# Moving the row-sum products of the norm behind the output products of their slot

## The chip, the cores and the metric

One Trainium2 chip, one core. The metric is the device time of one execution in microseconds (us). Timed runs of the kernel before gave a median of 982.25 us (979.91 to 983.06, 3 runs).

Names of engines in the lines of the profile: PE is TensorE's products, PEld its weight loads, DVE is VectorE, ACT is ScalarE, POOL is GpSimd.

## The reference

A Fourier filter along the sequence, then a gated feed-forward network with an RMS norm in front:

```
X = rfft(x, axis=1)                      # x: 8 x 3008 x 256
y = irfft(X * (filt_r + i filt_i))       # per batch
rms = sqrt(mean(y*y, axis=-1) + 1e-6)
xn  = y / rms * rms_g
out = (silu(xn @ w_gate) * (xn @ w_val)) @ w_out     # 256 -> 1536 -> 256
```

The norm needs, for each of the 3008 positions of each of the 8 batches, the sum of 256 squares. The kernel takes these sums on TensorE, as products of the squares with a column of ones. They are the row-sum products of the title.

## The kernel before

After a start-up, the kernel runs 576 slots: 8 batches, 6 tiles (m) of up to 512 positions, and 12 column blocks (jt) of the hidden layer. A slot is `gv` (gate and value products, into pg and pv) for the slot itself and `down` (output products, into po) for the slot two before it. Between them stand the units of the Fourier filter of later batches, which are laid into the slots by a plan. One of these units is `q_unit`, the row sums:

```python
psM = ctx.enter_context(tc.tile_pool(name="psM", bufs=1, space=bass.MemoryType.PSUM))
psB = ctx.enter_context(tc.tile_pool(name="psB", bufs=1, space=bass.MemoryType.PSUM))
...
def b_unit(b, i):                        # filter products, into psb: the one buffer of psB
    ps = bank(3 if b else (0, 1, 3)[i % 3], "psb").rearrange("p (a d) -> p a d", a=2)
    ...
        if b > 1:
            nc.vector.tensor_tensor(out=s1, in0=ps, in1=f1, op=ALU.mult)      # L223
            st[b]["s"][i] = (s1, s2, ps, f2)
            return
    ...
def swap_unit(b, i, h):                  # reads psb one (h = 0) and two (h = 1) slots later
    ...
    nc.vector.tensor_tensor(out=s2[a], in0=ps[e], in1=f2[e], op=ALU.mult)     # L243
    if h:
        ...
        nc.gpsimd.tensor_tensor(out=s, in0=s1, in1=s2, op=ALU.add)            # L246
...
def q_unit(b, m):
    sq = st[b]["sq"].pop(m)
    ps = psB.tile([P, 4], FP32, tag="mb", name="psq")     # the same buffer as psb
    for q in range(4):
        for dh in range(2):
            nc.tensor.matmul(ps[:, q:q + 1], sq[:, dh, ts(q, P)], ones,       # L304
                             start=(dh == 0), stop=(dh == 1))
    ...
    nc.vector.tensor_scalar(out=u, in0=ps, ...)                               # L308
    nc.gpsimd.tensor_tensor(out=rho, in0=u, in1=mhalf, op=ALU.pow)            # L310
...
for i in range(len(items) + 4):          # the slots
    if i < len(items):
        gv(*items[i])
    for fn, a in plan.get(i, ()):        # units: psa, psq, psi, psb, psn ...
        fn(*a)
    if 2 <= i < len(items) + 2:
        down(*items[i - 2])              # po; at jt == 11 also the copies of po to o
```

For batches from 2 on, psb is written every fourth slot. It has three readers on DVE, in that slot and the next two: a product with f1, and two "swap" products, each of one half of psb with f2 (h = 0, then h = 1, the second swap). psq comes in the slot after. psq of batches 1 to 6 therefore meets psb of the batch after, 36 times. Other units: psa (first stage of the transform, of two batches later), psi (inverse filter products), psn (last stage of the inverse).

## Time and profile before

| | before |
|---|---|
| time, median | 982.25 us |
| busy: PE, DVE, ACT, POOL | 91%, 68%, 64%, 38% of the span |
| weight loads of psq that waited for DVE's second swap | 36 times, 32.0 us |
| last pv to psq, start to start, waited / not waited | 0.78 / 0.216 us |

The head of the page of before, with the busy time, share of the span and number of instructions of each engine:

```profile
span 986.1 us, 17361 instructions
## 1 busy us (share of the span) xinstructions
PE 896.9 (91%) x6095; PEld 555.3 (56%) x6095; DVE 669.7 (68%) x1047; ACT 632.9 (64%) x1066; POOL 377.2 (38%) x325
```

TensorE is the limit, so what counts is where it stands still. The lists of waits of before, of the products and of the weight loads, tell who waited for whom: total us, times, longest.

```profile
engine line waited for: us in total, times, longest us
PE psq L304 <- DVE s L243: 14.7, 36, 0.5
...
PE psi L255 <- POOL s L246: 2.5, 7, 0.5
...
PE psb L215 <- DVE u L308: 0.4, 1, 0.4
```

```profile
engine line waited for: us in total, times, longest us
PEld L304 <- DVE s L243: 32.0, 36, 0.9
```

The timeline of before shows one of the 36 (start, duration, engine, line, operation; in brackets the idle time before it and what ended it):

```profile
319.04 0.59 PE L382 MATMUL pv<-xn,wv 128*128 128x512 f16 x2
...
319.30 0.68 DVE L243 TENSOR_TENSOR s<-psb,fi 64x512 f16<-64x512 f32 x1
320.01 0.69 DVE L387 TENSOR_TENSOR hh<-pv,sg 128x512 f16<-128x512 f32 x1
320.03 0.27 PEld L304 LDWEIGHTS <-sq 128*128 128x128 f16 x8 [0.89 <-DVE s L243]
320.04 0.35 PE L304 MATMUL psq<-ones,sq 128*128 128x1 f16 x8 [0.40 <-DVE s L243]
...
320.25 0.38 PE L194 MATMUL psa<-xc,wa 128*128 128x512 f16 x1
320.25 0.53 PEld L398 LDWEIGHTS <-hh 128*128 128x128 f16 x4
320.47 0.60 PE L398 MATMUL po<-wo,hh 128*128 128x256 f16 x4
```

The swap ends at 319.98 and psq starts at 320.04. The two pv products start 0.22 us apart, so the next product could have started at about 319.48. The wait costs 0.56 us, more than the 0.40 us that the list books, because the list counts from the end of a product and a pipelined successor starts before that end. Meanwhile the psa and po products, which need nothing from the swap, stand in line behind psq. The chain of waits of before says the same: it leaves TensorE here and runs over ACT and DVE.

```profile
317.94 0.61 ACT sg L386
318.55 0.02 issue
318.57 0.69 DVE hh L387
319.26 0.03 issue
319.30 0.69 DVE s L243
319.99 0.05 issue
320.04 0.35 PE psq L304 x8
320.39 0.24 PE psa L194
320.63 0.44 PE po L398 x4
```

### The profile page before, as it was taken

To read this page: it belongs to the slowest core of one execution; us is meant where nothing else is said; L and a number is where in the kernel's file an instruction comes from. 1 tells how busy PE (TensorE), PEld (TensorE's weight loads), DVE (VectorE), ACT (ScalarE), POOL (GpSimd) and SP (SyncE) were. 2 spreads that over 40 slices of the span, in tenths; PEclk is the share of its full clock that TensorE was granted. 3 is DMA by queue.
4 is the path that set the end of the run, shared out by engine and by line. 5 is a ranking of instruction groups with operands and counts; after the bars stand their busy time and mean duration, and the time that the engine had idled before them with its cause. 6 is when DMAs were issued, how large, how long until landed. Compare 5 with 4: busy or idle time off the path is not lost.

```text
span 986.1 us, 17361 instructions
## 1 busy us (share of the span) xinstructions
PE 896.9 (91%) x6095; PEld 555.3 (56%) x6095; DVE 669.7 (68%) x1047; ACT 632.9 (64%) x1066; POOL 377.2 (38%) x325
## 2 busy tenths in 40 slices
PE   3446978899999999999999999999999999999997
PEld 1223545565555656666666656666666666666654
DVE  6623444577777777777777878777777878555554
ACT  7333666677756776677766776577756765566543
POOL 3564334435441445325552445234431444033200
PEclk8556999999999999999999999999999999999999
DMA  8869574663457444764456434732345323422211
GB/s 194 150 124 175 130 167 99 149 173 86 92 111 164 85 101 92 162 129 90 91 117 158 108 78 92 173 101 73 76 106 130 87 60 68 116 44 62 44 44 41
DMA packets 94839, 106.99 MB, mean 108 GB/s; under 512 B 17112, under 2 KB 69464, under 8 KB 94560
## 3 DMA queue, kind: packets, MB, share of 16 engines
q1 hardware_dynamic: 85104, 87.92, 37.5%
q0 software_dynamic: 9552, 17.77, 11.8%
q8 instruction: 48, 0.79, 0.4%
q14 instruction: 39, 0.32, 0.1%
q10 hardware_dynamic: 96, 0.20, 0.1%
HBM read 70.62 MB, written 49.90 MB: 122 GB/s over the span
## 4 chain that ended last, share of the span: by engine, by line
PE 72%; DVE 8%; DMA 7%; issue 4%; ACT 4%; POOL 3%; SPq 0%; DVEq 0%; POOLq 0%; ACTq 0%
PE po L398 22%; PE pg L382 21%; PE pv L382 19%; DVE hh L387 4%; DVE s L243 3%; PE psi L255 3%; ACT sg L386 3%; PE psb L215 2%; DMA fi<-in_filt_i_dram 2%; PE psn L286 2%; PE psa L194 2%; PE psq L304 1%; DMA z_tmp<-t 1%; DVE o L404 1%; DMA wv<-in_moe_w_val_dram 1%
## 5 line engine op out<-in xcount | busy, mean ns | idle before, releaser
L387 DVE TENSOR_TENSOR hh<-pv,sg 128x512 f16<-128x512 f32 (+1 forms) x576 | 391.7, 680 | 253.8 <-ACT sg L386 106.5
L386 ACT ACTIVATE sg<-pg 128x512 f16<-128x512 f32 (+1 forms) x576 | 338.7, 588 | 237.2 <-PE pg L382 221.0
L398 PE MATMUL po<-wo,hh 128*128 128x256 f16 x2304 | 350.3, 273 | 1.7
L382 PE MATMUL pg<-xn,wg 128*128 128x512 f16 (+1 forms) x1152 | 341.2, 378 | 0.0
L382 PE MATMUL pv<-xn,wv 128*128 128x512 f16 (+1 forms) x1152 | 340.7, 378 | 0.0
L398 PEld LDWEIGHTS <-hh 128*128 128x128 f16 x2304 | 219.6, 98 | 107.1 <-issue 14.5
L246 POOL TENSOR_TENSOR s<-s,s 128x512 f16<-128x512 f16 x96 | 110.6, 1152 | 377.4 <-DVE s L243 340.5
L382 PEld LDWEIGHTS <-wv 128*128 128x128 f16 x1152 | 113.5, 99 | 133.3 <-issue 4.4
L367 POOL TENSOR_TENSOR xn<-y,rb 128x1024 f16<-128x1024 f32 x46 | 132.1, 2871 | 53.6 <-DMA rb<-r_tmp 53.6
L243 DVE TENSOR_TENSOR s<-psb,fi 64x512 f16<-64x512 f32 x192 | 132.1, 688 | 6.0
L382 PEld LDWEIGHTS <-wg 128*128 128x128 f16 x1152 | 113.0, 98 | 14.2 <-issue 0.6
L260 ACT ACTIVATE t<-psi 96x512 f16<-96x512 f32 x128 | 75.6, 592 | 24.7 <-PE psi L255 13.3
L196 ACT ACTIVATE t<-psa 128x512 f16<-128x512 f32 x96 | 56.4, 602 | 29.7 <-PE psa L194 24.3
L291 ACT ACTIVATE y<-psn,gsb 128x512 f32<-128x512 f32 x94 | 64.6, 687 | 13.7 <-PE psn L286 5.8
L310 POOL TENSOR_TENSOR rho<-u,mhalf 128x4 f32<-128x4 f32 x48 | 49.0, 1022 | 56.0 <-DVE u L308 55.9
L255 PEld LDWEIGHTS <-wi 128*128 128x128 f16 x320 | 33.5, 106 | 58.7 <-issue 22.4
L223 DVE TENSOR_TENSOR s<-psb,fr 128x512 f16<-128x512 f32 x96 | 65.4, 682 | 0.7 <-PE psb L215 0.2
L215 PE MATMUL psb<-t,wb 96*128 96x256 f16 x256 | 52.6, 290 | 7.6 <-DMA t<-z_tmp 6.1
L296 ACT ACTIVATE sq<-psn 128x512 f16<-128x512 f32 x94 | 55.6, 592 | 0.0
L255 PE MATMUL psi<-s,wi 128*128 128x256 f16 x256 | 46.6, 274 | 6.9 <-ACT sq L296 3.9
L194 PE MATMUL psa<-xc,wa 128*128 128x512 f16 x96 | 37.5, 405 | 16.7 <-DMA xc<-in_x_dram 8.8
L286 PEld LDWEIGHTS <-t 128*128 128x128 f16 x376 | 29.3, 99 | 22.5 <-issue 1.9
(60 smaller groups left out, 387.9 us busy)
## 6 DMA issues: line engine op xcount, KB each, us to landing
out_dram<-o SPq DMA_DIRECT2D x88, 256.0 KB, 3.3
z_tmp<-t SPq DMA_DIRECT2D x128, 96.0 KB, 2.3
t<-z_tmp SPq DMA_DIRECT2D x32, 384.0 KB, 5.0
g_tmp<-t SPq DMA_DIRECT2D x64, 192.0 KB, 3.2
t<-g_tmp SPq DMA_DIRECT2D x126, 96.0 KB, 2.7
rb<-r_tmp SPq DMA_DIRECT2D x46, 256.0 KB, 4.2
xc<-in_x_dram POOLq DMA_DIRECT2D x56, 192.0 KB, 5.9
out_dram<-o SPq DMA_DIRECT2D x8, 192.0 KB, 3.0
```

The costliest lines, as they stand in the source:

```text
L215: nc.tensor.matmul(ps[:, u, :], wb[:, k, :], st[b]["t2"][k // KC][:, k % KC, :], start=True, stop=True)
L223: nc.vector.tensor_tensor(out=s1, in0=ps, in1=f1, op=ALU.mult)
L243: nc.vector.tensor_tensor(out=s2[a], in0=ps[e], in1=f2[e], op=ALU.mult)
L246: nc.gpsimd.tensor_tensor(out=s, in0=s1, in1=s2, op=ALU.add)
L255: nc.tensor.matmul(ps[:, u, :], wi[:, 2 * i + u, q, :], ss[q][:, u, :], start=(q == 0), stop=(q == n - 1))
L260: nc.scalar.activation(out=st[b]["t3"][c][:, 2 * r:2 * r + 2, :], in_=ps[0:KR], func=AXT.Copy)
L291: nc.scalar.activation(out=y[:, dh, :], in_=ps, func=AXT.Identity, scale=gsb[:, dh:dh + 1])
L367: nc.gpsimd.tensor_tensor(out=xv, in0=yv, in1=rv.unsqueeze(1).to_broadcast([P, 2, 4, P]), op=ALU.mult)
L382: nc.tensor.matmul(ps[:, 0:w], wt[:, dt_, ts(jt, P)], xn[:, dt_, 0:w], start=(dt_ == 0), stop=(dt_ == 1))
L386: nc.scalar.activation(out=sg[:, 0:w], in_=pg[:, 0:w], func=AXT.Silu)
L387: nc.vector.tensor_tensor(out=hh[:, 0:w], in0=pv[:, 0:w], in1=sg[:, 0:w], op=ALU.mult)
L398: nc.tensor.matmul(po[s4 // 2][:, s4 % 2, :], hh[:, ts(s4, P)], wo[:, jt, :], start=(jt == 0 and s4 % 2 == 0), stop=(jt == JT - 1 and s4 % ...
```

## The change

The intent is to let ready work pass the row sums: psq and its DVE reader u are emitted at the end of the slot, behind the other units and behind po.

```diff
-        plan = {}
+        plan, late = {}, {}
 
         def at(slot, fn, *a):
-            todo = plan.setdefault(slot, [])
+            todo = (late if fn == q_unit else plan).setdefault(slot, [])
...
                 down(*items[i - 2])
                 if items[i - 2][2] == JT - 1:
                     stores[i + 1] = items[i - 2][:2]
+            for fn, a in late.get(i, ()):
+                fn(*a)
             if i in stores:
                 o_store(*stores[i])
```

No instruction is added or removed.

## The prediction

> **What bounds it now.** TensorE: the page has PE busy 91% of the span, DVE 68%, ACT 64%; the chain of waits is 72% PE. From 300 us on the timeline shows it streaming almost without a gap: a slot is two pg and two pv products (0.22 us from start to start), extra units, then four po products (0.44 us together). The largest wait of this steady part is the one that the change touches: in the list of waits, weight loads of the row-sum products (psq) waited 32.0 us for DVE s (the second swap product), 36 times; PE is booked idle 14.7 us there. "PSUM — Partial Sum Buffer" of the Trainium skill, section Terms, says that a bank is 2 KiB per partition; psq and the filter product psb share the one such buffer of their pool, so psq may not write before the swap has read psb. The trace agrees: the swap ends at 319.98, psq starts at 320.04.
>
> **What the wait costs.** From the start of the last pv to the start of psq it takes 0.78 us where psq waits and 0.216 us where it doesn't. So each of the 36 waits costs 0.56 us: 20 us, 2.1% of the run.
>
> **What the change does.** No instruction is added or removed. psq and its DVE consumer u go behind the slot's other units and po. Work of 0.44 us (po), or 0.66 us where the slot also holds a psa, fills the wait.
> - 20 of the 36 slots (batches 1 to 5) hold a psa: 0.56 us each, 11.2 us.
> - Batch 6 has none: four slots keep 0.13 us, gain 0.43 each, 1.7 us.
> - In 12 slots po also ends a tile. There u now stands behind the DVE copy of o (0.68 us, or 0.42 + 0.41), and the next slot's psb needs the buffer that u reads. hh (0.69), copy and u (0.15) end 1.5 to 1.7 us after the swap, so psb starts almost when it did: gain 0.05 to 0.2 each, 1.4 us, and a new wait "psb for DVE u", 0.2 to 0.4 us each.
> - Batch 1: psi waits for the POOL addition (1.15 us), partly behind xn (2.87 us), whose start hangs on the DMA of rho. PE coming earlier waits there: minus 1.5 us.
> - Batch 0: two slots (near 131 and 178 us) hold a psb of batch 1, now in front of psq, which then waits for two DVE products of 0.68 us: minus 1.0 and 0.8 us; another slot wins 0.2.
>
> Later rho costs little elsewhere: xn is needed several slots later, and the first use of rho (95 us) waits for POOL, held by weight DMAs.
>
> **Sum.** 11.2 + 1.7 + 1.4 - 1.5 - 1.6 = about 11 us of the 20. Predicted 971 us, range 965 to 976. Faster by over 2% (below about 963) 0.07, within 2% 0.92, slower 0.01.
>
> **What would show it.** In the list of waits "psq for DVE s" falls from 14.7 us to below 3 (weight loads: from 32 to below 10); "psb for DVE u" rises from 0.4 to 3 to 5 us. Busy times and counts stay. In a slot with psa the next pg starts 0.56 us sooner after the last pv. The gain is even over batches 2 to 6, small in batch 1, zero in batch 7, negative in batch 0.
>
> **What would make it wrong.** If ACT or DVE, which caught up during these waits, become the next limit, the gain is smaller. If u behind the copy delays psb less than worked out, it goes towards 15 to 18 us. If psq between po and the next pg exposes weight loads that were hidden, some 0.1 us for each of 48 units is lost.

## The result, and the profile after

The kernel after took 969.0 us (967.03 to 969.92, 4 runs) beside 982.55 us for the kernel before (979.91 to 983.06, 4 runs). The ratio is 0.9865, with a 95% interval of 0.984 to 0.9889: 1.35% less time, clear of noise but within 2%. Ratios here are the mean time of one kernel's fast runs over that of the other's of the same rounds, so not quite the ratio of the quoted medians. Run again later, the kernel after took 967.41 us (5 runs), a ratio of 0.9852 (0.9826 to 0.9878).

The head of the page of after:

```profile
span 966.1 us, 17361 instructions
## 1 busy us (share of the span) xinstructions
PE 884.5 (92%) x6095; PEld 553.0 (57%) x6095; DVE 668.8 (69%) x1047; ACT 632.9 (66%) x1066; POOL 376.8 (39%) x325
```

In the list of the products' waits of after, psq no longer waits for L243 at all. Two short waits for L237, in batch 0, are new. The list of the weight loads keeps a remainder:

```profile
engine line waited for: us in total, times, longest us
...
PE psi L255 <- POOL s L246: 3.4, 9, 0.6
...
PE psq L304 <- DVE s L237: 1.0, 2, 0.7
```

```profile
PEld L304 <- DVE s L243: 3.9, 16, 0.3
```

The same slot in the timeline of after:

```profile
313.51 0.59 PE L382 MATMUL pv<-xn,wv 128*128 128x512 f16 x2
...
313.77 0.68 DVE L243 TENSOR_TENSOR s<-psb,fi 64x512 f16<-64x512 f32 x1
313.95 0.38 PE L194 MATMUL psa<-xc,wa 128*128 128x512 f16 x1
...
314.16 0.60 PE L398 MATMUL po<-wo,hh 128*128 128x256 f16 x4
...
314.60 0.34 PE L304 MATMUL psq<-ones,sq 128*128 128x1 f16 x8
...
314.80 0.59 PE L382 MATMUL pg<-xn,wg 128*128 128x512 f16 x2
```

The swap still ends about 0.94 us after the first pv starts, as before (319.98 - 319.04 and 314.45 - 313.51). But psa and po now run in that time, and psq finds its buffer free. From the first pv of this slot to the first pg of the next it takes 1.29 us here; before it took 1.86 us (the next pg of before starts at 320.90). The chain of waits of after stays on TensorE:

```profile
313.68 0.43 PE pv L382 x2
314.11 0.22 PE psa L194
314.33 0.44 PE po L398 x4
314.76 0.18 PE psq L304 x8
314.94 0.45 PE pg L382 x2
```

To place the gain, I took from each trace the start of the gate activation (sg) of every slot and subtracted. A second trace of each kernel shows how far such a stage repeats:

| stage (slots) | before | before, again | after | after, again |
|---|---|---|---|---|
| 0 to 40 | 88.3 | 84.1 | 82.0 | 80.2 |
| 40 to 54 | 27.59 | 27.60 | 28.38 | 28.54 |
| 54 to 72 | 28.94 | 28.93 | 28.63 | 28.45 |
| 72 to 144 | 113.52 | 113.50 | 111.47 | 111.35 |
| 144 to 216 | 109.91 | 109.90 | 106.93 | 106.92 |
| 216 to 288 | 109.90 | 109.91 | 106.93 | 106.92 |
| 288 to 360 | 109.91 | 109.89 | 106.93 | 106.93 |
| 360 to 432 | 108.61 | 108.61 | 105.95 | 105.94 |
| 432 to 504 | 103.68 | 103.67 | 102.15 | 102.13 |
| 504 to 575 | 94.38 | 94.38 | 94.24 | 94.24 |

From slot 72 on, stages repeat within 0.15 us, and from slot 144 within 0.02 us. The gains there add up to 15.3 us (2.05 + 2.98 + 2.97 + 2.98 + 2.66 + 1.53 + 0.14). The first 40 slots wait for loads from memory and scatter by several us between executions of one kernel; the trace of before with its span of 986.1 us had an unluckily long start. Part of it is TensorE's granted clock: in the trace of before it is 0.63 of full speed from 142 to 145 us and 0.66 from 151 to 154 us, and products start up to 0.43 us apart there instead of 0.22. The second trace of before has one such stretch there, those of after have none; whether the change has to do with that is not shown. So the 20 us between the two spans is not the gain. The timed 13 to 15 us is, and what the first 72 slots contribute to it can't be told to better than some 2 us.

### The profile page after: what moved, and what is told of

Read it like the earlier page. It is cut to its first block, busy times and chain, and to the rows that moved or that the text cites. A ratio compares the mean times of both kernels' runs of the same rounds, so it can differ in the third digit from the quotient of the medians.

```text
span 966.1 us, 17361 instructions
## 1 busy us (share of the span) xinstructions
PE 884.5 (92%) x6095; PEld 553.0 (57%) x6095; DVE 668.8 (69%) x1047; ACT 632.9 (66%) x1066; POOL 376.8 (39%) x325
## 4 chain that ended last, share of the span: by engine, by line
PE 77%; DMA 8%; issue 5%; POOL 4%; DVE 4%; ACT 2%; SPq 0%; POOLq 0%; DVEq 0%; ACTq 0%
PE po L398 23%; PE pg L382 22%; PE pv L382 21%; PE psi L255 3%; PE psb L215 2%; DMA fi<-in_filt_i_dram 2%; PE psn L286 2%; PE psa L194 2%; DMA rb<-r_tmp 2%; DVE hh L387 1%; POOL s L246 1%; DVE o L404 1%; PE psq L304 1%; DMA wv<-in_moe_w_val_dram 1%; DMA xc<-in_x_dram 1%
## 5 line engine op out<-in xcount | busy, mean ns | idle before, releaser
L246 POOL TENSOR_TENSOR s<-s,s 128x512 f16<-128x512 f16 x96 | 110.7, 1153 | 358.7 <-DVE s L243 296.8
L243 DVE TENSOR_TENSOR s<-psb,fi 64x512 f16<-64x512 f32 x192 | 132.1, 688 | 6.0
L382 PEld LDWEIGHTS <-wg 128*128 128x128 f16 x1152 | 109.2, 98 | 12.6 <-issue 0.6
```

The source lines that it names most:

```text
L382: nc.tensor.matmul(ps[:, 0:w], wt[:, dt_, ts(jt, P)], xn[:, dt_, 0:w], start=(dt_ == 0), stop=(dt_ == 1))
```

## The experiments

The expectations below speak of "batches 2 to 5" and 106.1, 106.9 or 106.3 us each. That holds for the slots of batches 2 to 4; the slots of batch 5 (360 to 432) take about 1 us less in every kernel, which I had overlooked, so I compare batches 2 to 4.

My theory: the gain is the wait for psb's buffer, filled by the products that were moved in front of psq, and nothing else. Two rivals: the new place of psq or po in the stream of TensorE is worth something of its own (weight loads hidden or bared, buffers released sooner); or the gain comes from other engines' work starting earlier.

The traces of before and after speak against the second rival. Taken slot by slot, from the first pg to the first pg of the next slot, in batches 2 to 4 (slots 144 to 360) only the six slots of each batch with a psq are shorter: by 0.57 us with a psa (0.61 in the tile of 448 columns), by 0.43 without. The slots right behind the two in which po ends a tile are 0.14 and 0.08 us longer. No other slot differs by more than 0.01 us, and the second traces give the same.

### Take away the wait, keep the order

```diff
-                todo.insert(0, (fn, a))
+                todo.insert(len([f for f, _ in todo if f == swap_unit]), (fn, a))
...
-                    at(s0 + 2, swap_unit, b, i, 1)
+                    at(s0 + 1, swap_unit, b, i, 1)
```

This is the kernel before with the second swap one slot earlier, right behind the first (the changed insert keeps the two in order). psq stays in front of po.

> The order of before, psq in front of po, but the second swap product moved one slot earlier, behind the first, so that the bank is free long before psq. If the wait for the bank is the whole cost: psq waits for DVE s fall from 36 to none, all 20 us of the waits are won (more than the change's 13), and psi of batch 2 waits less for the POOL addition too: about 960 us. If instead the gain of the change came from where po or psq stand in the TensorE stream (weight loads, an earlier release of buffers), nothing is won: 980 us or more. If DVE with three products in one slot becomes the limit: above 985 us.

Measured: 956.14 us (4 runs), ratio 0.9723 (0.9685 to 0.9761). A second set gave 956.19 us (5 runs), ratio 0.9734 (0.9703 to 0.9765):

> The order of before with the early second swap once more, the fastest version so far, beside the other on one chip: 955 to 958 us, batches 2 to 5 at 106.1 us each, the stage of slots 40 to 54 at 27.6 us as in before (psq of batch 0 in front).

The list of the products' waits holds no line of psq for L243 and none of psi for the POOL addition (L246); the weight loads of psq keep 1.2 us for L243, 7 times. (The second trace has one wait for the addition, 0.8 us, before slot 72.) The stage of slots 72 to 144 takes 106.42 us and each of the next three 106.1 us, 0.8 us less than after. The second trace repeats this to 0.02 us. Its stage of slots 40 to 54 took 28.68 us instead of the expected 27.6, with the order of before: that stage too can differ by a us by chance.

The cause is shown: with the order of before untouched, freeing the buffer earlier wins all that the change won and more. This run also starts the addition on POOL earlier, so the slots have to be told apart. From slot 72 on it wins 24.7 us: 19.7 us in the 34 slots with a psq, 0.57 us in each (0.61 with 448 columns); 3.6 us in other slots of batch 1, where psi no longer waits for POOL; 1.4 us in others, which I did not follow up. DVE with three products in one slot was no limit.

### Half of the move

```diff
+            for fn, a in late.get(i, ()):
+                fn(*a)
             if 2 <= i < len(items) + 2:
                 down(*items[i - 2])
...
-            for fn, a in late.get(i, ()):
-                fn(*a)
```

> psq behind the slot's other units but still in front of po: half of the change. If the gain is just the work that stands between and fills the wait: 20 slots with a psa gain 0.22 us each, 4.4 us, and batch 0 loses about 1.6 as in the change: about 979 to 980 us, and in the trace psq still waits 0.56 us in slots without psa and 0.34 us with. If only the place behind po matters: 982 to 984 us. If any move backwards is enough: 969 us.

Measured: 980.94 us (4 runs), ratio 0.9978 (0.9936 to 1.0021), a little above the 979 to 980 expected and not to be told from before by its time. The trace tells it: the list of waits has all 36 again, shorter in total than the 14.7 us of before.

```profile
PE psq L304 <- DVE s L243: 10.3, 36, 0.5
```

In slots with a psa, psa to psq takes 0.56 us from start to start, where the psa stream itself takes 0.22: a wait of 0.34 us, as expected. Without psa, pv to psq takes 0.78 us as before. Batches 2 to 4 take 108.98 us each, 0.92 us less than before; four times 0.22 is 0.88. So the gain is the amount of work placed in front of psq, up to the length of the wait.

### Both together: the place of psq when there is nothing to fill

This is the change with the earlier second swap, both diffs from above.

> The change and the earlier second swap together. Theory: the move behind po is worth only the wait that it fills; with the bank free early there is none to fill, so the place of psq is worth nothing: the run's time within 2 us of the run with the early swap alone (956 us), batches 2 to 5 within 0.2 us of its 106.1 us each. Rival: standing between po and pg has a gain (or a cost) of its own, such as weight loads hidden or bared: batches differ by 0.6 us (0.1 us in each of six slots) or more, in either direction.

Measured: 958.46 us (5 runs), ratio 0.9758 (0.9733 to 0.9783). Batches 2 to 4 take 106.34 us each against 106.13 with the early swap alone. The move on top of the early swap wins nothing; it costs about 0.2 us per batch. The bounds that I had set (0.2 us per batch, 2 us in all) were both just missed, so I looked for those 0.2 us. In the two slots of each batch in which po ends a tile, the DVE reader u stands behind the copies of o, and the next psb waits for u: it starts 0.36 and 0.31 us after psi instead of 0.22. The timeline of this kernel, such a slot:

```profile
334.00 0.41 DVE L406 COPY o<-po 128x256 f32<-128x256 f32 x1
...
334.33 0.41 DVE L407 COPY o<-po 64x256 f32<-64x256 f32 x1
...
334.66 0.14 DVE L308 TENSOR_SCALAR u<-psq 128x4 f32<-128x4 f32 x1
334.86 0.38 PE L215 MATMUL psb<-t,wb 96*128 96x256 f16 x2
```

The next kernel splits the copies of o off `down`, so that in these slots they are issued behind psq and u:

```diff
+    def evacuate(b, m, jt):
+        po = po_of[(b, m)]
         if jt == JT - 1:
...
                 down(*items[i - 2])
...
             for fn, a in late.get(i, ()):
                 fn(*a)
+            if 2 <= i < len(items) + 2:
+                evacuate(*items[i - 2])
```

> Early second swap and psq behind po, but in the slots where po ends a tile the copies of o are issued behind psq, so that u stands in front of the DVE copy. Theory: the 0.22 us per batch that psq behind po cost with the early swap (106.34 against 106.13) are psb waiting for u behind the copy, in two slots of each batch: batches 2 to 5 return to 106.13 within 0.05. If they stay at 106.3 or more, the cost is the place of psq among the products itself. The whole: 956 to 959 us.

Measured: batches 2 to 4 take 106.11, 106.11 and 106.12 us, those of the early swap alone. The whole took 958.95 us (5 runs, ratio 0.9748, 0.9724 to 0.9772). The slots behind the copy slots are back to psi and psb 0.22 us apart. The cost was u behind the copy. The place of psq among the products is worth nothing in either direction (0.02 us in 72 slots), and the first rival falls. This kernel and the previous one are still some 2 us slower than the early swap alone in the medians. The stages from slot 72 on don't show that, so it lies in the first 72 slots, where psq of batch 0 was also moved. With the scatter of that part I don't call its cause shown.

### Batch 0 left as it was

```diff
-            todo = (late if fn == q_unit else plan).setdefault(slot, [])
+            todo = (late if fn == q_unit and a[0] else plan).setdefault(slot, [])
```

> The change for batches 1 to 7 only; psq of batch 0 stays in front as before. Theory: the change loses in batch 0, where psb of batch 1 now stands ahead of psq (0.9 and 0.4 us seen in the trace of after); keeping batch 0 wins 1 to 1.5 us: about 967.5 us, and every stage from the 72nd slot on takes what it takes in after to 0.1 us. Rival: batch 0 gained too (its slots 22 to 72 were 1.3 us shorter in the trace of after): 970 us or more.

Measured: 967.75 us (965.32 to 971.22, 4 runs), ratio 0.9845 (0.98 to 0.989). The stages from slot 72 on are those of after within 0.15 us. The median is where it was expected, but the intervals of this kernel and of after overlap almost wholly, so the time decides nothing. Single slots decide more. Slot 42 holds one of the two psq that the prediction named for batch 0 (near 178 us). It takes 2.99 us in all five traces with psq of batch 0 in front (before twice, early swap twice, this one), and 3.42 us in the traces of after, e5_lag6, e6_early_and_late and e7_u_before_copy, where psq stands behind po and waits 0.41 us. So the change loses 0.43 us here. What else the stage of slots 40 to 54 varies by, the stray 28.68 above too, is mostly in slot 50, where psb waits for its load (in the list of waits: 0.2 and 0.4 us in the traces of after, 0.9 in the second one of the early swap).

### More distance still

psq goes between the pg and the pv products of the next slot, 0.43 us further back:

```diff
-    def gv(b, m, jt):
+    def gv(b, m, jt, mid=()):
...
                                  start=(dt_ == 0), stop=(dt_ == 1))
+            for fn, a in mid if ps is pg else ():
+                fn(*a)
...
-                gv(*items[i])
+                gv(*items[i], mid=late.get(i - 1, ()))
```

> The change, with psq another two products later, between pg and pv of the next slot: 0.43 us more work in front of it. Theory: the 16 slots without psa, which keep a wait of 0.125 us each, lose it: batches 2 to 5 gain 0.25 us each (106.7 instead of 106.93), batch 6 and 7's stages about 0.7 us together, less what psb then waits for u (0.04 us in the trace of after, up to 0.2 here): 967 to 969 us. Rival: more distance goes on helping: below 964 us. If u now comes too late for psb: batches longer than in after.

Measured: 966.77 us (4 runs), ratio 0.9838 (0.9805 to 0.9871), at the lower edge of what was expected. No psq of batches 1 to 6 waits any longer (0.19 to 0.22 us from pg to psq). The stages of slots 360 to 432 and 432 to 504 are shorter by 0.32 and 0.26 us, together close to the expected 0.7. But batches 2 to 4 stay at 106.92, not the 106.7 that I expected. Their two slots without psa are those with the copies on DVE; there the next psb waits for u, and u's turn on DVE doesn't depend on whether TensorE came 0.13 us sooner: psb starts 0.50 and 0.45 us after psi here, 0.37 and 0.31 in after, 0.22 where it doesn't wait. (The 0.04 us in the expectation was misread: the delay in after is 0.15 and 0.09 us.) The wait changed its owner. This part of the expectation missed.

### The waits of batch 1 for POOL

In batch 1 (slots 72 to 144) the change won 2.05 us, less than the 2.98 us of its neighbours. I held psi's waits for the POOL addition responsible, and gave psi two more slots:

```diff
-                lag, t4_at, n_at = 4, 118, 123
+                lag, t4_at, n_at = 6, 118, 123
```

> The change, and in batch 2 the inverse products psi come 6 slots after psb instead of 4. Theory: in batch 1 the time that the change gave was partly lost to psi waiting for the POOL addition (16 waits, together 6.7 us beyond an unwaited start in the trace of after): with two more slots most of them vanish, batch 1 takes about 106 instead of 111.5 us, the whole 963 us. Rival: batch 1 gained less for another reason (DMA, clock): 968 us or more.

Measured: 974.89 us (4 runs), ratio 0.9911 (0.9859 to 0.9964), slower than after. The stage took 114.60 us instead of 111.47. The waits for the addition are gone from the list, but a larger one stands in their place:

```profile
PE psi L255 <- ACT sq L296: 12.8, 15, 1.3
```

Two slots later psi falls into the slot in which ACT still squares psn out of the only buffer of the pool psM, which psi needs. It is the same fault as psq's, in the other pool: a ready product stands in line for a bank whose reader is late. The run doesn't refute the reason for batch 1's smaller gain. The early swap speaks for it: it starts the addition a slot sooner without moving psi, psi waits for POOL no more in this stage, which takes 106.42 us, close to its neighbours. The trace of after shows it directly, in the bullet on batch 1 below.

### Second traces

> The kernel after once more, for its scatter and a second trace: 967 to 970 us; stages from slot 72 on within 0.2 us of the first trace; the first 22 slots, which wait for DMA, may differ by several us.

> The kernel before once more, for a second trace: stages from slot 72 on within 0.2 us of the first trace; if the first 72 slots of the first trace (145 us) were long by chance, this one shows some 138 to 142 us.

Both came as expected for the stages from slot 72 on (0.15 us or better). The first 72 slots of before took 140.6 us in the second trace (84.1 + 27.6 + 28.9) and 144.8 us in the first: the first was long by chance.

## Why the prediction was right or wrong

The prediction was right: 971 us with a range of 965 to 976, measured 969.0 and later 967.4. One of its terms, that for the copies of o, was well off.

- **The wait and its price.** Predicted: 36 waits of 0.56 us, 20 us, for the buffer that psq shares with psb. The early swap took these waits away and won 0.57 us in each slot with a psq (0.61 with 448 columns), beside some us elsewhere. Right.
- **Slots with psa.** Predicted: the wait vanishes, 20 times 0.56 us. In after, po to psq takes 0.109 us in every such slot, which is the stream of one po product. Right.
- **Batch 6.** Predicted: 0.13 us of wait remains and 0.43 us are won in each of four slots. Measured: 0.235 us from po to psq instead of 0.109, so 0.126 us remain. The 2.66 us of slots 360 to 432 are four slots of batch 5 and two of these. Right.
- **The 12 slots with the copy of o.** Predicted: 0.05 to 0.2 us each, 1.4 us in all, and 3 to 5 us of "psb for DVE u" in the list. Measured: a batch won 2.98 us. Its four slots with psa account for about 2.3 (three of 0.57, and one of 0.61 in the tile of 448 columns), so the two others won about 0.33 each (0.43 in the slot, less 0.14 or 0.08 in the next), about 4 us over 12 slots. The delay of psb is 0.15 us behind the two short copies and 0.09 behind the long one, not 0.2 to 0.4, and the line "psb for DVE u" never appeared: the list counts from the end of psi, 0.38 us after its start, and psb starts before that. This is the term that was mis-sized. The mechanism was right, as the split of `down` showed, but I added whole durations (0.69 + 0.42 + 0.41 + 0.15). The section "Optimizing Scalar/DVE Operations" of "Perfetto Trace Analysis", in the Trainium skill, says that part of an instruction's profiled latency overlaps with the next instruction. The traces agree in kind. The timeline of after, DVE alone, in such a slot:

```profile
337.73 0.69 DVE L387 TENSOR_TENSOR hh<-pv,sg 128x512 f16<-128x512 f32 x1
338.34 0.41 DVE L406 COPY o<-po 128x256 f32<-128x256 f32 x1
338.67 0.41 DVE L407 COPY o<-po 64x256 f32<-64x256 f32 x1
339.00 0.14 DVE L308 TENSOR_SCALAR u<-psq 128x4 f32<-128x4 f32 x1
```

  and the products of the next slot that wait for it, from the timeline of all engines:

```profile
338.83 0.38 PE L255 MATMUL psi<-s,wi 128*128 128x256 f16 x2
...
339.20 0.38 PE L215 MATMUL psb<-t,wb 96*128 96x256 f16 x2
```

  Each on DVE starts 0.08 us before the duration of the one in front is over: 0.61, 0.33 and 0.33 us from start to start. u ends at 339.14, 1.41 us after hh began, not 1.67. With so little to wait for, being 0.26 us off was most of the term.
- **Batch 1.** Predicted: minus 1.5 us, psi waiting for POOL. Measured: the stage of slots 72 to 144 won 0.9 us less than its neighbours, and psi's waits for POOL rose from 2.5 to 3.4 us in the list (2.9 in the second trace). In four slots right behind a psq slot (78, 86, 94, 102) psi starts 0.72, 0.24, 0.17 and 0.16 us later after pv than in before, 1.3 us in all, and each time 0.05 us after the end of the POOL addition; two more such slots (62 and 70) lie before slot 72. Right, and of about that size.
- **Batch 0.** Predicted: minus 1.0 us near 131 us and minus 0.8 us near 178 us. The second is there with half the size: 0.43 us in slot 42. Of the first, the wait is there: psq of slot 24 waits 0.89 us behind po in both traces of after. What it costs is not to be told: TensorE waits there for the load of psb in both kernels, and slots 0 to 40 scatter by several us.
- **What would have made it wrong.** ACT and DVE did not become the limit, and no weight load was bared: with the buffer free, psq in front of po or behind it gave the same time to 0.02 us per 72 slots.

The sum came out 2 to 4 us too small in gain, mostly because of the term for the copies (about 4 us instead of 1.4); the loss near 178 us, 0.43 instead of 0.8, goes the same way.

## What to carry to other kernels

When a product waits for a buffer, look first at who holds the buffer, and only then at the order in which products stand: reordering won 13 to 15 us by hiding the wait under 0.44 to 0.66 us of other work, while letting the last reader go one slot earlier removed the wait and won 26 us (956 us), some 20 of them from this wait, with one number changed in the plan and a line that keeps the two swaps in order. "Perfetto Trace Analysis" of the Trainium skill, section "Optimization Strategy", says that the same gap repeating on the engine that should be saturated can mean too little PSUM for the next tile; the 36 gaps of about 0.56 us here were that, in that psq shares the one buffer of its pool with psb. No run gave psq a buffer of its own. And when you cost a queue of short instructions, take the distance between their starts from the trace and not the sum of their durations.

## What the Trainium skill lacked or had wrong

- "TensorE: Matmul & The Clock Gate", Architectural detail: it says that TensorE's queue can pull weight loads ahead of running products, but not what a waiting weight load does to those behind it. In before, psq's load waited up to 0.9 us for DVE, and the loads of psa and po behind it, which needed nothing from DVE, started only after it (320.03, then 320.25 for po). In none of the 36 cases did a later load start before psq's.
- "Perfetto Trace Analysis", Optimizing Scalar/DVE Operations: it gives about 125 ns of access overhead for DVE on PSUM and says that as much again, in the profiled latency, overlaps with the next instruction. Here consecutive products and copies from PSUM to SBUF, of 0.41 to 0.69 us, overlapped by 0.08 us. That is less than 0.125 us; which figure the page means for an instruction that reads PSUM and writes SBUF it doesn't say.
- "Perfetto Trace Analysis", Tensor Engine Instruction: it says that the end of a product is estimated. It doesn't say what follows for waits: the idle time booked for psq was 14.7 us, where the starts show 36 times 0.56, about 20 us; and psb's delay of 0.15 us behind u was not booked at all.
